# Sparse attention and a gated mixture layer on one core: seven products instead of eight in the outputs of two superblocks, and one written order for all engines

## The chip, the cores and the metric

The kernel runs on one core of one Trainium2 chip. The metric is the device time of one execution in microseconds (us); lower is better. The core's engines are TensorE (PE in the profile, with its weight loads as PEld), VectorE (DVE), ScalarE (ACT), GpSimd (POOL) and SyncE (SP), which here only issues transfers. Each engine runs its own instructions in program order and waits for the others where it needs their data or a buffer.

## What is computed

Eight batches of eight heads of attention over 576 positions, with two masks, then a gated layer over all 4608 tokens of width 512.

```python
mask_local = (rel >= 0) & (rel < stride)                                   # heads 0 to 3, stride 32
mask_strided = (rel >= 0) & (pos[None, :] % stride == pos[:, None] % stride)  # heads 4 to 7
scores = np.where(masks[None, :, :, :], scores, -1000000000.0)
attn = np.exp(scores - np.max(scores, axis=-1, keepdims=True))
attn = attn / (np.sum(attn, axis=-1, keepdims=True) + 1e-09)
x = np.matmul(attn, v)                       # 4608 x 512, heads side by side
gate = 1.0 / (1.0 + np.exp(-(x @ w_gate)))   # w_gate, w_val 512 x 1536
out = gate * (x @ w_val) @ w_out             # w_out 1536 x 512
```

## The kernel before

**Precision.** A float32 matrix is kept as two fp32r parts: h, a rounded copy (a cast on ACT), and l, what is left (a subtraction on DVE or POOL). A product of two such matrices is three products of parts (h·h, h·l, l·h; `three`, L417, and `outs`, L448). A large product in this text is one matmul of 128x128 weights against 512 columns.

**First block.** Batch 0, 512 of its 576 tokens, goes through the layer by plain products: for each of the 12 chunks of 128 hidden units, gate and value (24 products) and outputs (12), 432 in all. Beside it the attention of batches 0 to 2 runs, and the weights come in: `load_weight` (token W) fetches them as 64-bit words, ACT and DVE turn the words into float32 (a, b: `upper_words` and `lower_words`; w: `whole`, L390 to L399, a shift and an addition), and u and l split them (L407, L410). The last 64 tokens of each batch, the rests, are put aside.

**Superblocks.** The remaining batches go in pairs: `SUPER = ((1, 2), (3, 4), (5, 6), (7, None))`, where None stands for the eight rests together; a block is 512 tokens. Per superblock the two blocks' inputs are combined into seven input matrices, and gate and value weights into seven mixes, as in Winograd's form of Strassen's method, so that two halves of the tokens and two halves of the features need seven products (P1 to P7) instead of eight. `pair_of_chunks` (L559) does this for six pairs of chunks: 14 steps of 6 large products, 84 steps and 504 products. The results are combined by DVE and ACT (L571 to L573, L589 to L591) into h1 and h2, the gated hidden values. Mixes are formed by `form_mix` (L502) in the first superblock, kept in DRAM and loaded again in the later ones into a ring of four tiles (`next_of_ring`).

**Outputs.** Then `group_of_outs` (L618) makes the outputs of the two blocks by plain products, in 8 groups of three chunks: `load_outs` (L604) loads the output weights of a group (1.5 MB, already split) into the same ring, `split_outs` (L611) splits the hidden values (L615 on ACT, L616 on DVE), and 12 products per chunk follow, tokens on the partitions: 48 steps of 6, 288 products. `store` (L455) copies the four results of a block from PSUM (L459 on DVE, L461 on ACT) and writes rows of 2 KB.

**What sets the order.** All code runs in one manual schedule, so each engine's instructions stand in the order in which the Python issues them. For the first block and the attention beside it the string `ORDER` gives one token for each action; its parts between bars belong to the first steps of the first superblock. From there on `superblock` plans: `put` enters an action before or beside one of 132 steps (`tick`). `FORM` says at which steps the mixes are formed, and one pair of heads of the next superblock's attention gets 14 steps, with `STEP` and `TURN_AT` (turnings of the probabilities, L261, eight a pair of heads). The inputs of the next superblock (`mix_input`, L345: T are sums at L353, h casts at L363, l rests at L365, L the same on POOL) come in the last steps of the outputs.

**Attention of a pair of heads:** scores on PE (L197), mask, maximum and difference on DVE, exponential on ACT (L227), sum, the addition of 1e-9 and the reciprocal (`inverse`), multiplication by it (L240), turning by blocks (L261) and weighing on PE (L289).

```python
    def outs(accs, h, w, first, last, start=0):
        hh, hl = h
        wh, wl = w
        for i, o in enumerate(accs, start):
            for n, (a, b) in enumerate(((hh, wh), (hh, wl), (hl, wh))):
                nc.tensor.matmul(o, a[:, i * P : (i + 1) * P], b, start=first and n == 0, stop=last and n == 2)
```

Here the hidden values are the matmul's weights and the output weights move, so the outputs come out by tokens.

Of the kernel before, what the change touches and what calls it, by code (L numbers as in the profile page):

```python
# [65 lines left out]
ORDER = """  # L66
Q00 Z00 Z01 C Q01 S00 C1 W0.0 F000 F100 S01 F200 W0.1 E00 F001 N000 Q02 a0.0 F101 b0.0 N100 F201 a0.1 W1.0 N200 E01
w0.0 T00 b0.1 P00 Q03 w0.1 u0.0 Z02 S02 N001 l0.0 u0.1 F002 a1.0 V00 l0.1 b1.0 N101 F102 N201 V01 F202 T01 w1.0 E02
W1.1 P01 N002 X00 u1.0 Z03 M0- W0.2 S03 H00 N102 l1.0 L00 F003 V02 R00 g0.1.0 a1.1 N302 X01 F103 b1.1 g0.0.0 H01 w1.1
a0.2 V03 T02 L01 b0.2 U1.1 P02 F203 W2.0 g0.1.1 R01 Z10 w0.2 X02 E03 N003 l1.1 W2.1 g0.0.1 H02 N103 g1.0.0 L02 U0.2  # L70
N203 Q11 R02 g0.1.2 a2.0 D0.2 g1.0.1 b2.0 T03 w2.0 a2.1 W1.2 g1.0.2 P03 g1.1.0 u2.0 Z11 X03 b2.1 l2.0 g1.1.1 H03 V11
g0.0.2 L03 g1.1.2 w2.1 a1.2 W2.2 g0.0.3 R03 b1.2 S11 U2.1 s0 w1.2 g1.0.3 W3.0 g1.1.3 F011 l2.1 g0.1.3 F111 Q13 g2.0
U1.2 a2.2 m0 b2.2 F211 s1 w2.2 x0 W3.1 a3.0 g2.1 E11 y0 D1.2 V10 U2.2 m1 b3.0 l2.2 N011 O0 x1 N111 s2 Y1 W3.2 w3.0
a3.1 O1 b3.1 N311 m2 u3.0 x2 W4.0 D3.0 a3.2 w3.1 b3.2 T11 g3.0 P11 W4.1 w3.2 u3.1 Z13 Y2 Q10 a4.0 D3.1 X11 s3 U3.2
b4.0 g3.1 H11 l3.2 V13 a4.1 R11 w4.0 b4.1 W4.2 S10 w4.1 u4.0 O2 W5.0 D4.0 u4.1 m3 D4.1 x3 F010 Q12 Y3 a4.2 g4.1 F110
b4.2 w4.2 a5.0 W5.1 F210 b5.0 S13 u4.2 w5.0 E10 W5.2 g4.0 F013 D4.2 u5.0 Q21 N010 a5.1 D5.0 O3 b5.1 N110 s4 F113 W6.0
N210 w5.1 a5.2 T10 b5.2 m4 g5.0 P10 W6.1 w5.2 x4 Z12 u5.1 y4 a6.0 D5.1 b6.0 S12 F213 s5 W6.2 w6.0 g5.1 E13 F012 U5.2
Q20 D5.2 u6.0 F112 a6.1 X10 D6.0 b6.1 a6.2 F312 m5 g6.0 H10 N013 W7.0 x5 N113 b6.2 w6.1 E12 W7.1 R10 w6.2 u6.1 O4 s6
# [838 lines left out]
```

## Time and profile before

| | |
|---|---|
| median of 3 runs | 962.56 us (960.55, 962.56, 964.04) |
| the profiled execution | 959.72 us, of which the span is 957.9 us |
| mean granted TensorE clock | 0.993 |
| moved by DMA | 212.83 MB, 222 GB/s over the span |
| transfers to landing, median | gate and value mixes (1 MB) 9.3 us, output weights (1.5 MB) 6.4 us, an output of 256 KB 2.4 us |
| table loads on ACT | 46 |

The span runs from the first to the last instruction; the time of an execution has something around it. A row of the groups of instructions gives line, engine, operation, out<-in by the program's names (hs are split hidden values, wo output weights, mix the mixes, pt turned probabilities), shapes and count, then busy time in us and mean ns of one, then the engine's idle time just before and what ended it. A row of the stretches gives the stretch, its length and the busy time (and instructions) of PE, PEld, DVE, ACT and POOL, the granted clock, the share of time the DMA engines were busy, and GB/s. Matmuls overlap in the pipeline, so a mean of 392 ns for one does not say that one starts every 392 ns.

### The profile page before, as it was taken

The numbers are of one execution on the slowest core, as the hardware profiler recorded it, in microseconds if no ns is written. First come the engines' busy times: TensorE is split into PE (matmuls) and PEld (weight loads), VectorE is DVE, ScalarE is ACT, GpSimd is POOL, SyncE is SP. The second block draws the span as 40 slices with busy tenths as digits, with TensorE's granted clock in tenths as the row PEclk, the third lists the DMA queues.
The fourth block names the chain that finished last, engine by engine and source line by source line (L and its number), as shares of the span: only waits on it lengthen the run. The fifth ranks groups of instructions, "written<-read, shape, count | busy, mean of one in ns | idle before, by whom it ended". The sixth has DMA issues, their size and how long they took to land.

```text
span 957.9 us, 18020 instructions
## 1 busy us (share of the span) xinstructions
PE 924.3 (96%) x7576; PEld 744.2 (78%) x7576; DVE 583.8 (61%) x900; ACT 436.2 (46%) x778; POOL 112.5 (12%) x120
## 2 busy tenths in 40 slices
PE   3999999999999999999999999999999999999997
PEld 3778777677777878888777788877888888888886
DVE  6789888888877575566668674666266122224221
ACT  4679776756564333454443243444344123333121
POOL 1341345364430000000000000000000000000000
PEclk9999999989999999999999999999999999999999
DMA  7788765655573576865525669455625585531563
GB/s 267 234 301 282 263 242 210 238 229 227 199 260 139 212 271 245 321 252 231 213 109 185 218 234 374 197 221 212 215 103 213 199 342 217 239 159 66 198 242 111
DMA packets 43825, 212.83 MB, mean 222 GB/s; under 512 B 8672, under 2 KB 9952, under 8 KB 33504
## 3 DMA queue, kind: packets, MB, share of 16 engines
q1 hardware_dynamic: 40544, 199.77, 55.7%
q10 hardware_dynamic: 3200, 11.91, 3.7%
q8 instruction: 60, 0.98, 0.4%
q14 instruction: 21, 0.17, 0.1%
HBM read 172.86 MB, written 38.80 MB: 221 GB/s over the span
## 4 chain that ended last, share of the span: by engine, by line
PE 75%; DVE 13%; ACT 6%; DMA 3%; issue 2%; POOL 1%; SPq 0%; DVEq 0%; ACTq 0%; POOLq 0%
PE o L420 30%; PE o L453 13%; PE g L420 6%; PE g L453 6%; PE v L453 6%; PE v L420 6%; PE x L289 3%; PE s L197 2%; DVE pt L261 2%; DMA first_x1h<-in_w_all 2%; DMA first_x1l<-in_w_all 1%; ACT L227 1%; ACT mix L532 1%; DVE hs L616 1%; DVE mix L537 1%
## 5 line engine op out<-in xcount | busy, mean ns | idle before, releaser
L453 PE MATMUL o<-wo,hs 128*128 128x512 f32 x576 | 148.2, 392 | 0.9 <-DVE ob L459 0.9
L453 PEld LDWEIGHTS o<-wo,hs 128*128 128x128 f32 x576 | 107.2, 188 | 26.6 <-DVE ob L459 2.3
L616 DVE TENSOR_TENSOR hs<-h,hs 128x512 fp32r<-128x512 f32 x96 | 63.9, 688 | 104.4 <-ACT hs L615 104.2
L572 DVE TENSOR_TENSOR h<-s,o 128x512 f32<-128x512 f32 x48 | 32.9, 685 | 98.9 <-PE o L420 96.9
L615 ACT CAST hs<-h 128x512 fp32r<-128x512 f32 x96 | 55.3, 618 | 74.6 <-PE o L453 47.4
L261 DVE STREAM_TRANSPOSE pt<-sb 32x320 f32<-32x320 f32 (+1 forms) x160 | 85.8, 536 | 4.8
L453 PE MATMUL g<-wo,hs 128*128 128x512 f32 x288 | 81.9, 393 | 0.0
L573 ACT ACTIVATE s<-s 128x512 f32<-128x512 f32 x48 | 30.4, 633 | 111.7 <-DVE s L571 111.7
L453 PE MATMUL v<-wo,hs 128*128 128x512 f32 x288 | 81.0, 389 | 0.0
L420 PE MATMUL o<-x,mix 128*128 128x512 f32 x288 | 71.8, 397 | 0.2 <-ACT vq L591 0.2
L420 PE MATMUL o<-x0h,mix 128*128 128x512 f32 x192 | 67.6, 413 | 3.9 <-DVE ob L459 2.0
L420 PEld LDWEIGHTS o<-x,mix 128*128 128x128 f32 x288 | 52.9, 188 | 15.5 <-ACT s L573 3.2
L420 PE MATMUL o<-x2h,mix 128*128 128x512 f32 x192 | 64.5, 397 | 0.4
L420 PE MATMUL o<-x3h,mix 128*128 128x512 f32 x192 | 63.3, 390 | 0.3 <-DVE h L572 0.3
L420 PE MATMUL o<-x6h,mix 128*128 128x512 f32 x192 | 63.0, 389 | 0.0
L453 PEld LDWEIGHTS v<-wo,hs 128*128 128x128 f32 x288 | 54.1, 188 | 11.4
L453 PEld LDWEIGHTS g<-wo,hs 128*128 128x128 f32 x288 | 53.4, 188 | 11.2
L589 ACT COPY o<-o 128x512 f32<-128x512 f32 x48 | 27.4, 572 | 76.2 <-PE o L420 76.2
L231 DVE TENSOR_REDUCE mx<-sb 128x10 f32<-128x640 f32 (+1 forms) x26 | 21.3, 819 | 48.5 <-ACT sb L227 48.5
L420 PEld LDWEIGHTS o<-x0h,mix 128*128 128x128 f32 x192 | 37.4, 195 | 13.4 <-DVE ob L459 2.1
L573 ACT ACTIVATE s<-o 128x512 f32<-128x512 f32 x48 | 28.7, 598 | 34.8 <-PE o L420 34.6
L420 PEld LDWEIGHTS o<-x2h,mix 128*128 128x128 f32 x192 | 36.7, 191 | 9.4 <-ACT gq L591 1.7
(177 smaller groups left out, 1803.2 us busy)
## 6 DMA issues: line engine op xcount, KB each, us to landing
wo<-outer SPq DMA_DIRECT2D x32, 1536.0 KB, 6.4
mix<-mix SPq DMA_DIRECT2D x36, 1024.0 KB, 9.3
mix<-mix SPq DMA_DIRECT2D x36, 768.0 KB, 7.1
mix<-mix SPq DMA_DIRECT2D x12, 1792.0 KB, 6.0
first_x1h<-in_w_all SPq DMA_DIRECT2D x18, 512.0 KB, 4.7
first_x1l<-in_w_all SPq DMA_DIRECT2D x18, 512.0 KB, 4.6
out<-ob SPq DMA_DIRECT2D x32, 256.0 KB, 2.4
qk<-in_qk_l SPq DMA_DIRECT2D x11, 592.0 KB, 6.1
```

The source lines that it names most:

```text
L197: nc.tensor.matmul(sc[g * m : (g + 1) * m, j * BANK + s * kk : j * BANK + (s + 1) * kk], qk[d, q0 : q0 + m], qk[d, k0 : k0 + kk], start=Tr ...
L227: nc.scalar.activation(prob, prob, AF.Exp, scale=SCALE)
L231: nc.vector.tensor_reduce(row, prob, axis=AX.X, op=ALU.add)
L261: nc.vector.transpose(dst[to : to + LB, :, col : col + LB], src[rows : rows + LB, :, h * LB : (h + 1) * LB])
L289: nc.tensor.matmul(xp[j * D : (j + 1) * D, r * BANK + (u * per + g) * m : r * BANK + (u * per + g + 1) * m], v[rows, (u * per + g) * P + j ...
L420: nc.tensor.matmul(o, w, x, start=first and n == 0, stop=last and n == len(todo) - 1, skip_group_check=onto)
L453: nc.tensor.matmul(o, a[:, i * P : (i + 1) * P], b, start=first and n == 0, stop=last and n == 2)
L572: mul = lambda to, x, y: nc.vector.tensor_tensor(to, x, y, op=ALU.mult)
L573: sig = lambda to, x: nc.scalar.activation(to, x, AF.Sigmoid)
L589: P1=(g1, v1, lambda: nc.scalar.copy(g2, g1), lambda: nc.scalar.copy(v2, v1), True),
L615: nc.scalar.copy(hh, src)
L616: nc.vector.tensor_tensor(hl, src, hh.bitcast(F32), op=ALU.subtract)
```

## The change

1. **Outputs by seven products.** In the third and fourth superblocks (`BY_PARTS = (2, 3)`) `outs_by_parts` takes the place of `group_of_outs`. The hidden values of a pair of chunks are four matrices (A, B, C, D: two chunks by two blocks); `sum_of_h` makes the differences in place, and seven products, each in three stages of two pairs of chunks, give four quarters of the outputs: 7 x 3 x 2 steps of 6 products, 252. A stage is a ring tile with the output weights of one product (`load_stage`, two transfers of 256 KB) and the split hidden values (`split_stage`: casts on ACT, differences on DVE or POOL). The weights are now the stationary side and the hidden values move, so results come out with output columns on the partitions; DVE turns them in 32x32 blocks (`done`) and `store_turned` writes pieces of 256 bytes, four transfers a quarter for a batch and eight for the rests. The columns of `w_out` are permuted on the host (`turned`) so that turned blocks of 32 give whole runs; the plain `store` undoes the permutation in its copies (`runs`).
2. **Sums of the output weights.** `form_outs` makes the sums that the products need (tokens @l to @k: load, add up the halves, sums, casts, rests, keep), three pairs of chunks during the gates of the second superblock and three during those of the third, in the tiles of hidden chunks that are not yet written, and keeps them in DRAM.
3. **One written order.** `ORDERS` holds four texts, one for each superblock (the first with the first block ahead), with one part between bars for each step of six products; the planner (`FORM`, `STEP`, `TURN_AT`, `put`) goes. A token with @ is a step that the planner placed before; the last figure of @j and @T chooses DVE or POOL. The order of the first block is another one too.
4. **Smaller edits.** `inverse` becomes two steps (`safe`, `inverse`), and `whole` two (`shift`, `whole`); `load_mix` two transfers with places of their own; the temporary tiles are joined in twos; Q and V transfers from the fourth batch on go by SP's queue.

In the texts the attention beside the second superblock (batches 5 and 6) stands in steps 68 to 132 of 132, the first scores beside step 70; before, a pair of heads began every 14 steps from the first step on.

```diff
 SUPER = ((1, 2), (3, 4), (5, 6), (7, None))
+BY_PARTS = (2, 3)
+STAGE = 2
+STAGES = PAIRS // STAGE
+TURNED = 4
+OUT_SUMS = dict(P5=0, P6=1, P7=2, P3=3)
+OUT_PLAIN = dict(P1=(0, 0), P2=(1, 0), P4=(1, 1))
...
-ORDER = """
...
-X22 e3 e0 M1lt e2 e1 H22 | M1va R22 JT1 X23 M1vs Jh1 | M1ld H23 Jl1 R23 M1k S30 JT3 Jh4 | F030 Jh5 JT2 | Jl5 Jh3 | M2-
...
+ORDERS = (
+    """
...
+@J3.l2 @G2.16 @i2.16.0 @g2.16.1 @i2.16.1 | @T1.4.0 @g2.16.0 @G2.17 @i2.17.1 @j2.16.0.1 @i2.17.0 @g2.17.0 | @j2.16.1.1
...
+        def safe():
+            prob, row, by_row = rows()
+            nc.vector.tensor_scalar_add(row, row, 1e-9)
...
+    def shift(f, i):
+        high = words[f, i][0]
+        nc.vector.tensor_scalar(high, high, 3, None, op0=ALU.logical_shift_left)
...
+            (nc.vector.tensor_copy if i % 2 else nc.scalar.copy)(runs(ob, "a q"), runs(accs[i], "q a"))
...
-    def split_outs(s, n, q):
+    def split_outs(n, q, part, engine=None):
         j, g = divmod(n, GROUPS // 2)
         src = hs[g * THREE + q][:, j * TB : (j + 1) * TB]
         hh, hl = (hold["h", n][:, (2 * q + k) * TB : (2 * q + k + 1) * TB] for k in range(2))
-        nc.scalar.copy(hh, src)
-        nc.vector.tensor_tensor(hl, src, hh.bitcast(F32), op=ALU.subtract)
+        if part == 0:
+            nc.scalar.copy(hh, src)
+        else:
+            engine.tensor_tensor(hl, src, hh.bitcast(F32), op=ALU.subtract)
...
+    def form_outs(what, p, *args):
...
+        if what == "s":
+            t["st"] = flat("st", 4 * PART, f"sums_out{p}")
+            of = [t["st"][:, n * PART : (n + 1) * PART] for n in range(4)]
+            a11, a21, a12, a22 = (t["w"][:, n * PART : (n + 1) * PART] for n in range(4))
+            tt = (nc.gpsimd, nc.vector)[args[0]].tensor_tensor
+            tt(of[0], a21, a22, op=ALU.add)
+            tt(of[1], of[0], a11, op=ALU.subtract)
+            tt(of[2], a11, a21, op=ALU.subtract)
+            tt(of[3], a12, of[1], op=ALU.subtract)
+            return
...
+    def load_stage(n, q):
+        which, p = ORDER_OF_PARTS[n // STAGES], n % STAGES * STAGE + q
+        at = STAGE * 2 * TB + q * 2 * PART
+        to = hold["stage", n][:, at : at + 2 * PART].bitcast(F32)
+        if which in OUT_SUMS:
+            at = OUT_SUMS[which] * 2 * PART
+            nc.sync.dma_start(to, sums_out[p][:, at : at + 2 * PART])
+        else:
+            odd, half = OUT_PLAIN[which]
+            f = 2 * p + odd
+            src = outer[f // THREE][:, f % THREE * 2 * DM : (f % THREE + 1) * 2 * DM]
+            src = src.rearrange("p (k n) -> p k n", k=2)[:, :, half * PART : (half + 1) * PART]
+            nc.sync.dma_start(to.rearrange("p (k n) -> p k n", k=2), src)
...
+    SPLIT_OF = dict(P1="A", P5="B", P6="B", P2="C", P7="A", P3="D", P4="B")
...
+    def split_stage(n, q, part, engine=None):
...
+        if part == 0:
+            nc.scalar.copy(h, src)
+        else:
+            engine.tensor_tensor(l, src, h.bitcast(F32), op=ALU.subtract)
...
+    def sum_of_h(p, m, engine):
+        a, b, c, d = (part_of_h(p, x) for x in "ABCD")
+        to, x, y = ((b, b, a), (b, d, b), (a, b, a), (b, c, b))[m - 1]
+        engine.tensor_tensor(to, x, y, op=ALU.subtract)
...
+    def store_turned(t, b, half, split):
+        for a in range(TURNED):
+            src = t[a * LB : (a + 1) * LB]
+            cols = slice(a * P + half * REST, a * P + (half + 1) * REST)
+            queue = nc.scalar if split and a % 2 else nc.sync
+            if b is not None:
+                to = out[b * S : b * S + TB, cols].rearrange("(m i) n -> i m n", i=LB)
+                queue.dma_start(to, src.rearrange("p (m n) -> p m n", n=REST))
...
+    def outs_by_parts(s, banks, tick):
+        (a1, a2, a5), (b1, b2, b5) = banks
+        one, two, five = (a1, b1), (a2, b2), (a5, b5)
...
+        def done(which, n, b, half, src, d):
...
+            nc.vector.transpose(to, src.rearrange("p (m j) -> p m j", j=LB))
...
+        after = dict(
+            P1=lambda d: nc.scalar.copy(two[d], one[d]),
+            P5=lambda d: keep("p", "t4", five, d),
+            P6=lambda d: keep("q", "t3", two, d),
+            P2=lambda d: done("P2", 0, 0, 0, one[d], d),
+            P7=lambda d: done("P7", 1, 1, 1, add("p", two, d), d),
+            P3=lambda d: done("P3", 2, 1, 0, add("q", five, d), d),
+            P4=lambda d: done("P4", 0, 0, 1, two[d], d),
+        )
+        into = dict(P1=one, P5=five, P6=two, P2=one, P7=two, P3=five, P4=two)
...
+            for k in range(STAGES):
+                t = hold.pop(("stage", i * STAGES + k))
+                for d in range(2):
+                    with tick():
+                        todo = []
+                        for q in range(STAGE):
+                            w, h = STAGE * 2 * TB + q * 2 * PART + d * P, 2 * q * TB
+                            wh, wl = (t[:, w + m * PART : w + m * PART + P] for m in range(2))
+                            todo.append(((wh, wl), (t[:, h : h + TB], t[:, h + TB : h + 2 * TB])))
+                        three(into[which][d], todo, fresh and k == 0, k == STAGES - 1, onto=not fresh)
+                    if k == STAGES - 1:
+                        after[which](d)
...
-                args = (nc.sync if b == 0 and (kind == "Q" or p < 2) or (b, p) == (BY_PE, 1) else nc.scalar,)
+                early = b == 0 and (kind == "Q" or p < 2)
+                args = (nc.sync if early or (b, p) > (BY_PE, 0) else nc.scalar,)
...
-    FORM = (
...
-    STEP = ((1, "F1"), (2, "F2"), (3, "E"), (5, "N0"), (6, "N1"), (6, "N2"))
-    TURN_AT = (7, 8, 9, 10, 11, 12, 13, 14)
...
+        def steps():
+            for what in order[clock[0]]:
+                step(what)
+            clock[0] += 1
...
+        if parts:
+            outs_by_parts(s, banks, tick)
+        else:
+            for n in range(GROUPS):
+                group_of_outs(s, n, banks, tick)
...
+    turned = w_out.reshape(DF, TURNED, TURNED, LB).transpose(0, 2, 1, 3)
-    w_all = np.stack([wg, wv, w_out.reshape(NF, P, DM)], 2).view(np.int64)
+    w_all = np.stack([wg, wv, turned.reshape(NF, P, DM)], 2).view(np.int64)
```

**TensorE, the outputs of the third superblock.** The rows are line, operation, out<-in with the tile's number, size and count; g, v, o_0 and o_1 are PSUM banks, wo and hs the loaded weights and split hidden values of a group. Before, a run in the change from the first group to the second:

```order
L453 MATMUL g3_5935<-wo3_0_6918,hs3_0_6917 128x512 x3
L453 MATMUL v3_5936<-wo3_0_6918,hs3_0_6917 128x512 x3
L453 MATMUL o3_0_5933<-wo3_0_6918,hs3_0_6917 128x512 x3
L453 MATMUL o3_1_5934<-wo3_0_6918,hs3_0_6917 128x512 x3
L453 MATMUL g3_5935<-wo3_1_7039,hs3_1_7038 128x512 x3
L453 MATMUL v3_5936<-wo3_1_7039,hs3_1_7038 128x512 x3
```

After, from the start of the same outputs (stage is a ring tile with weights and hidden values):

```order
L530 MATMUL o3_0_5931<-stage3_0_6773 128x512 x6
L530 MATMUL o3_1_5932<-stage3_0_6773 128x512 x6
L396 MATMUL x7_2_7011<-pt7_2_6912,vv7_2_6909 64x32 x36
L530 MATMUL o3_0_5931<-stage3_1_6796 128x512 x6
L530 MATMUL o3_1_5932<-stage3_1_6796 128x512 x6
L530 MATMUL o3_0_5931<-stage3_2_6982 128x512 x6
L530 MATMUL o3_1_5932<-stage3_2_6982 128x512 x6
L530 MATMUL g3_5933<-stage3_3_6997 128x512 x6
L530 MATMUL v3_5934<-stage3_3_6997 128x512 x6
L530 MATMUL g3_5933<-stage3_4_7048 128x512 x6
```

Each step's six products now go into one bank from one stage instead of two banks of three, and the weighings of batch 7 (x7) stand between them.

**VectorE, the fourth pair of chunks of the second superblock.** h2, s22, s12 and o2 are hidden values, gate sums and PSUM of that superblock; sb5, mx5 and pt5 belong to the attention of batch 5. Before:

```order
L219 TENSOR_REDUCE mx5_3_4673<-sb5_3_4672 128x12
L223 TENSOR_TENSOR sb5_3_4672<-sb5_3_4672,mx5_3_4673 128x12x54
L231 TENSOR_REDUCE mx5_3_4673<-sb5_3_4672 128x12
L235 TENSOR_SCALAR mx5_3_4673<-mx5_3_4673 128x12
L236 RECIPROCAL mx5_3_4673<-mx5_3_4673 128x12
L240 TENSOR_TENSOR sb5_3_4672<-sb5_3_4672,mx5_3_4673 128x12x54
L261 STREAM_TRANSPOSE pt5_3_4819<-sb5_3_4672 32x12x32
L572 TENSOR_TENSOR h2_6_4670<-s11_2_3_4811,o2_1_4062 128x512
```

After:

```order
L693 TENSOR_TENSOR h2_6_4446<-s11_2_3_4501,o2_1_4030 128x512
L692 TENSOR_TENSOR s22_2_3_4517<-o2_0_4029,gp_2_3_4469 128x512
L692 TENSOR_TENSOR s22_2_3_4517<-o2_1_4030,gp_2_3_4469 128x512
L692 TENSOR_TENSOR s12_2_3_4534<-g2_4031,gq_2_3_4484 128x512
L693 TENSOR_TENSOR h2_7_4447<-s22_2_3_4517 128x512
L692 TENSOR_TENSOR s12_2_3_4534<-v2_4032,gq_2_3_4484 128x512
L693 TENSOR_TENSOR h2_6_4446<-s12_2_3_4534 128x512
L693 TENSOR_TENSOR h2_7_4447<-s11_2_3_4501,o2_1_4030 128x512
```

The fourth pair of heads stood among the gates here; now the gates and values follow each other and the attention comes later.

**VectorE, the end of the outputs of the third superblock.** ob are copied outputs, turned3_P4 a turned quarter, raw and x inputs of the fourth superblock. Before:

```order
L616 TENSOR_TENSOR hs3_6_7305<-h3_6_6542,hs3_6_7305 128x512
L616 TENSOR_TENSOR hs3_6_7305<-h3_7_6543,hs3_6_7305 128x512
L616 TENSOR_TENSOR hs3_6_7305<-h3_8_6749,hs3_6_7305 128x512
L616 TENSOR_TENSOR hs3_7_7350<-h3_9_6750,hs3_7_7350 128x512
L616 TENSOR_TENSOR hs3_7_7350<-h3_10_6909,hs3_7_7350 128x512
L616 TENSOR_TENSOR hs3_7_7350<-h3_11_6910,hs3_7_7350 128x512
L459 COPY ob6_1_7434<-o3_1_5934 128x512
L459 COPY ob6_3_7440<-v3_5936 128x512
L572 TENSOR_TENSOR h4_0_7447<-s11_4_0_7507,o4_1_7444 128x512
L571 TENSOR_TENSOR s22_4_0_7522<-o4_0_7443,gp_4_0_7475 128x512
```

After:

```order
L829 TENSOR_TENSOR stage3_20_7462<-h3_10_6777,stage3_20_7462 128x512
L460 TENSOR_TENSOR raw7_5950<-raw_rest_7236,raw7_5950 128x1024
L460 TENSOR_TENSOR raw_rest_7236<-raw_rest_7236 128x1024
L866 STREAM_TRANSPOSE turned3_P4_7528<-o3_0_5931 128x16x32
L472 TENSOR_TENSOR x5_4_7525<-raw_rest_7236,x5_4_7525 128x1024
L460 TENSOR_TENSOR raw7_5950<-raw_rest_7236,raw7_5950 128x1024
L460 TENSOR_TENSOR raw7_5950<-raw7_5950 128x1024
L866 STREAM_TRANSPOSE turned3_P4_7528<-o3_1_5932 128x16x32
L693 TENSOR_TENSOR h4_0_7558<-s11_4_0_7616,o4_1_7555 128x512
L692 TENSOR_TENSOR s22_4_0_7631<-o4_0_7554,gp_4_0_7584 128x512
```

The differences of split hidden values stand alone before; after, one of them is followed by sums of the next inputs (L460), a rest (L472) and two turnings (L866) up to the last product.

More of the change, by code (lines that the diff above doesn't have):

```diff
@@ L64 @@
 }
-ORDER = """
[L67 to L76, printed above, removed]
@@ new lines, in sum_of_h @@
+    def sum_of_h(p, m, engine):
[10 more added lines that the diff above has]
+                queue.dma_start(to, src.rearrange("p (m n) -> p m n", n=REST))
+            else:
+                to = out.rearrange("(m r) n -> r m n", r=S)[TB:, :, cols]
+                for k in range(REST // LB):
+                    src_k = src.rearrange("p (m k n) -> p k m n", k=REST // LB, n=REST)[:, k]
+                    queue.dma_start(to[k * LB : (k + 1) * LB], src_k)
@@ L691, in step, with later_step @@
         elif kind == "e":
-            store(acc[0], 0, OBS[0], [int(of)])
+            store(acc[0], 0, ("t0", "t1", "t2", "t3"), [int(of)])
+    def later_step(kind, args):
+        if kind == "J":
+            mix_input(int(args[0]), args[1])
+            return
+        if kind == "O":
+            store_turned(*turned.pop(args[1]))
+            return
+        args = [int(x) for x in args if x]
+        engines = nc.vector, nc.gpsimd
+        if kind == "A":
+            room_of_mix(*args)
+        elif kind == "L":
+            load_mix(*args)
+        elif kind == "H":
+            load_outs(*args)
+        elif kind == "G":
+            room_of_stage(*args)
+        elif kind == "g":
+            load_stage(*args[1:])
+        elif kind in "ij":
+            split = split_stage if args[0] in BY_PARTS else split_outs
+            split(args[1], args[2], int(kind == "j"), engines[args[3]] if kind == "j" else None)
+        elif kind == "T":
+            sum_of_h(args[0], args[1], engines[args[2]])
+        elif kind == "R":
+            raw[None] = flat("raw_b", NC * TB, "raw_rest")
+            for m in range(B):
+                to = raw[None].rearrange("p (c n) -> p c n", c=NC)[:, :, m * REST : (m + 1) * REST]
+                nc.sync.dma_start(to, rests[m].rearrange("p (c n) -> p c n", c=NC))
+        else:
+            form_outs(kind, *args)
     forms = {}
@@ L807, in superblock @@
+    def superblock(s):
+        parts = s in BY_PARTS
+        order = [part.split() for part in ORDERS[s].split("|")]
         two = [bank(f"o{m}", f"o{s + 1}_{m}") for m in range(2)]
```

336 lines of the change are left out of this document (205 added, 131 removed).

## The prediction

> **What bounds the kernel now.** I read the page first: engine totals, then the chain that ended last.
>
> ```profile
> span 957.9 us, 18020 instructions
> PE 924.3 (96%) x7576; PEld 744.2 (78%) x7576; DVE 583.8 (61%) x900; ACT 436.2 (46%) x778; POOL 112.5 (12%) x120
> PE 75%; DVE 13%; ACT 6%; DMA 3%; issue 2%; POOL 1%; SPq 0%; DVEq 0%; ACTq 0%; POOLq 0%
> ```
>
> TensorE is in use almost throughout and is three quarters of the chain. A busy PE need not be a PE at its pace, so I took the pace from one piece of the chain in order of time, six large products in an undisturbed place, and then the busy times of each engine stage by stage. The columns are stretch, length, PE, weight loads, DVE, ACT, POOL (instructions in brackets), granted clock, DMA share and GB/s. I cut the stretches where the first block ends and where each superblock (a pair of batches) passes from its gate and value products to its outputs; the last row is what comes after the last product.
>
> ```profile
> 710.77 1.36 PE o L453 x6
> ```
> ```profile
> 0.00:163.80 163.80, 143.80 (x1925) 114.11 (x1925) 136.59 (x217) 118.33 (x221) 57.40 (x56) 1.00 0.75 258
> 163.80:306.00 142.20, 137.24 (x1317) 108.34 (x1317) 115.52 (x177) 84.70 (x154) 53.71 (x58) 0.97 0.54 210
> 306.00:379.60 73.60, 72.06 (x581) 57.89 (x576) 49.09 (x72) 24.86 (x47) 0.40 (x2) 1.00 0.67 248
> 379.60:508.90 129.30, 129.30 (x1201) 103.49 (x1192) 84.67 (x140) 59.57 (x100) 0.40 (x2) 1.00 0.56 217
> 508.90:582.60 73.70, 72.16 (x584) 57.92 (x577) 49.13 (x72) 24.86 (x47) 0.40 (x2) 1.00 0.67 249
> 582.60:706.40 123.80, 123.80 (x915) 100.15 (x913) 69.12 (x112) 52.25 (x92) 0.20 (x1) 1.00 0.56 211
> 706.40:772.20 65.80, 65.80 (x291) 53.99 (x289) 28.65 (x36) 20.31 (x32) 0.00 (x0) 1.00 0.61 224
> 772.20:886.40 114.20, 114.20 (x505) 94.59 (x504) 34.41 (x51) 37.94 (x66) 0.00 (x0) 1.00 0.49 193
> 886.40:952.10 65.70, 65.70 (x289) 53.72 (x288) 15.90 (x25) 12.78 (x23) 0.00 (x0) 1.00 0.50 184
> 952.10:957.90 5.80, 0.19 (x1) 0.00 (x0) 0.69 (x1) 0.59 (x1) 0.00 (x0) 0.78 0.61 182
> ```
>
> 1.36 us for six is 0.2267 us each. A superblock has 504 + 288 = 792 such products, 179.5 us. The fourth superblock (the two rows from 772.20) takes 179.9: it has no attention beside it and loses nothing. The third takes 189.6; the 9.7 more are the scores and weighings of four pairs of heads, 2.4 us a pair. The second, with eight pairs, takes 203.0 where 179.5 + 19.4 = 198.9 would do; the first takes 215.8 and loses 17. The first block needs 432 products, 97.9 us, plus twelve pairs, about 29, and takes 163.8: there DVE (136.6) and ACT (118.3) are nearly as full as PE. So from 379.6 on the time is the number of products; before that it is partly waits.
>
> **Fewer products.** The program's order shows 252 products where 288 stood in the outputs of the third and fourth superblocks: 42 steps of six instead of 48. That is 72 x 0.2267 = **-16.3 us**, all of it on PE where PE waits for nothing. It stands if the new work of the other engines stays hidden; the rest of this part is what hides it.
>
> **The work that feeds the products.** These are groups of instructions (line, engine, operation, out<-in, count; busy time, mean ns; idle before and its releaser).
>
> ```profile
> L616 DVE TENSOR_TENSOR hs<-h,hs 128x512 fp32r<-128x512 f32 x96 | 63.9, 688 | 104.4 <-ACT hs L615 104.2
> L615 ACT CAST hs<-h 128x512 fp32r<-128x512 f32 x96 | 55.3, 618 | 74.6 <-PE o L453 47.4 <-PE v L453 26.8
> L261 DVE STREAM_TRANSPOSE pt<-sb 32x384 f32<-32x384 f32 x80 | 45.6, 570 | 2.5
> L261 DVE STREAM_TRANSPOSE pt<-sb 32x320 f32<-32x320 f32 x80 | 40.2, 503 | 2.3
> L353 DVE TENSOR_TENSOR raw<-raw 128x1024 f32<-128x1024 f32 x7 | 9.0, 1290 | 0.5 <-ACT raw L320 0.4
> L365 DVE TENSOR_TENSOR x<-raw,x 128x1024 fp32r<-128x1024 f32 x6 | 7.3, 1218 | 0.0
> L412 POOL TENSOR_TENSOR w<-whole,w 128x512 fp32r<-128x512 f32 x9 | 11.9, 1333 | 27.8 <-ACT w L408 27.6
> ```
> ```profile
> wo<-outer SPq DMA_DIRECT2D x32, 1536.0 KB, 6.4
> ```
>
> ACT: 42 casts x 0.618 = 26 us in 57 us of products, with copies still far below PE. Loads: 42 of 256 KB (11.0 MB) a superblock where eight of 1536 KB (12.6 MB) were, asked for three or four stages (8 to 11 us) ahead against 6.4 us for six times the size. Both cost nothing; uncovered, a late stage would cost what it is late, a few us. The sums of the output weights are formed while the second and third superblocks make gates, where DVE has 40 us to spare; their stores end before the fourth pair of blocks writes the borrowed tiles. Also nothing, and 2 to 3 us if one store is late.
>
> DVE and POOL are the tight ones. A turned output is 512 elements; from 503 and 570 ns for 320 and 384 I estimate 704. A pair of attention heads costs DVE (69.12 + 28.65 - 34.41 - 15.90 - 13.7) / 4 = 8.5 us, the third superblock's DVE less the fourth's and less 4 x 1.29 + 7 x 1.22 for the next input sums and their rests (L353, L365). Counting the order by these prices:
> - last 42 steps of the third superblock: 57.1 + 2.4 = 59.5 us of PE; DVE 39 differences x 0.69 + 9 small turnings x 0.54 + 8 input sums and rests of about 1.25 + 8 turned outputs x 0.70 + 4 additions x 0.69 = 50; POOL 17 x 1.33 + 3 x 2.4 = 30 (2.4 us is the POOL row below).
> - last 56 steps of the second: 76.2 + 7 x 2.4 = 93 us of PE, because seven of eight attention pairs now stand there; DVE 7 x 8.5 + 24 = 84; POOL 13 x 1.33 + 5 x 2.4 = 29.
> - last 42 of the fourth: 57.1 us of PE; DVE 37, POOL 19. No excess.
>
> Alone each engine fits. Together they don't always run, as the order of time near 158 us shows:
>
> ```profile
> 157.61 0.42 DVE L525 TENSOR_TENSOR sums<-whole 128x256 f32<-128x256 f32 x1
> 158.00 2.40 POOL L365 TENSOR_TENSOR x2l<-raw,x2h 128x1024 fp32r<-128x1024 f32 x1 [2.96 <-ACT x2h L363]
> 158.06 2.61 DVE L526 TENSOR_TENSOR sums<-sums,whole 128x256 f32<-128x256 f32 x1
> ```
>
> The same subtraction took 0.42 us and, begun beside a POOL instruction, 2.61: it ended when POOL ended. [...]
>
> DVE plus POOL exceed PE by 20 us in each of the first two lists, 40 in all. The nearest row is 163.80:306.00, where 115.5 + 53.7 exceed 142.2 by 27 and PE lost 5.0, with about 3 more at half clock (below): 0.3 per us. Of the 40, some 8 at each superblock's end can run on into the next one's first steps, where DVE has little. So (40 - 16) x 0.3 = **+7 us**; bounds 0 and 40. A gain from these moves is excluded, as PE waits for nothing there now.
>
> **Waits before 379.6 that the order may move.** The largest waits of PE in 163.80:306.00 (us, times, longest), and what follows one:
>
> ```profile
> PE x L289 <- DVE pt L261: 2.2, 2, 1.8
> PE o L420 <- DVE ob L459: 2.0, 1, 2.0
> PE o L420 <- ACT s L573: 1.9, 1, 1.9
> ```
> ```profile
> 188.50:190.70 2.20, 0.33 (x25) 0.20 (x15) 0.72 (x3) 2.17 (x4) 0.00 (x0) 1.00 0.37 122
> 190.70:194.00 3.30, 3.30 (x8) 2.62 (x9) 3.23 (x8) 1.25 (x3) 0.75 (x2) 0.50 0.27 105
> ```
>
> In the second row eight products fill 3.3 us where fifteen would fit: the granted clock fell to 0.50 after 2 us of wait, so that wait cost 2 + 1.6. [...] Three waits and two such dips are 6.1 + 3.2 = 9.3 us. The order splits the two weight steps and the two reciprocal steps apart and groups ACT's functions (9 table loads for 13 in the first superblock), so some of this goes; I take a third, **-3 us**. Bounds: -12 with the smaller waits, +6 if the first block's other order waits as much anew, which no row excludes.
>
> **The end.** The last product and what follows it now, then the nearest rows for 256-byte pieces:
>
> ```profile
> 951.45 0.84 PE L453 MATMUL v<-wo,hs 128*128 128x512 f32 x3
> 952.33 0.69 DVE L459 COPY obNone<-v 128x512 f32<-128x512 f32 x1 [0.67 <-PE v L453]
> 953.01 1.39 ACTq L467 DMA_DIRECT2D out<-obNone  x2
> ```
> ```profile
> L801 SPq DMA_DIRECT2D raw_rest<-rests x8: 628/630/2524, 672.5 to 680.0; - x8
> DMA to landing us min/median/max: 2.7/5.0/6.8
> ```
>
> Now the last product ends at 952.29 and the program 5.6 us later. After: one turning (0.70), two issues on each queue (0.63, then 0.63), 5.0 to land, about 7.0: **+1.4 us**, bounds -1 and +3. The turned stores also pass SP's queue inside the outputs; 0.63 us an issue, four to eight of them, beside stage loads asked for 8 us ahead, cost nothing unless DVE is late with a turning, when the loads behind wait as long: part of the crowding above.
>
> **Sum.** -16.3 + 7 - 3 + 1.4 = -10.9. The profiled execution took 959.7 (span 957.9 and 1.8 around it), so 948.8; the median of the runs, 962.6, lies 2.8 above it: **951.7 us**.
>
> **Rivals.**
> [...]
> - [...] PE waits for the differences in the last 42 and 56 steps. All 40 us on PE: -16.3 + 1.4 + 40 - 3 = +22, 985 us; with 22.5 of them +4.6, 967 us. It decides from 17.9 us, 45% of the excess, where the nearest row shows 30%. For it: one 2 us wait costs 3.6. Against: stages are prepared 8 us ahead, so short delays vanish.
> - *Nothing left.* The excess costs 15 to 20 us and eats the gain: about 962.6.
> - That the change doesn't do what it says is out: the order has the 72 products fewer.
>
> **Chances.** Forecast 0.62 (own range 944 to 959), both gains 0.19, nothing left 0.09, lock 0.10. This kernel's runs tell about 0.3%, 2.9 us, from no change: faster 0.81, same 0.09, slower 0.10. The range, 936 to 964, leaves out the lock and little else: its low end is the first rival with the waits at -12 (-16.3 + 1.4 - 12 = -26.9, 935.7), its high end the excess at 20 us.
>
> **What would show it.** Outputs of the third and fourth superblocks in 57 to 60 us each with PE full: the first term right. PE waits on stage differences (DVE or POOL) near the ends of the second and third, and clock dips there: the crowding, with its size. [...] First product of the first superblock later than 163.8 us: the first block's order is worse. The forecast is wrong if the fourth superblock's outputs exceed 60 us, or if waits before 380 us change by over 8.

## The result, and the profile after

The changed kernel takes **969.12 us** (median of 5 runs, 967.26 to 971.5) beside 963.08 for the kernel before (5 runs): a ratio of 1.0064, 95% interval 1.0041 to 1.0088. It is slower by some 6 us; 951.7 was forecast, faster, and 969.1 lies above the range.

The head of the changed kernel's page and its chain, to be put beside those of before:

```profile
span 967.8 us, 18484 instructions
PE 912.4 (94%) x7504; PEld 733.7 (76%) x7504; DVE 609.6 (63%) x964; ACT 453.0 (47%) x820; POOL 242.1 (25%) x202
PE 84%; DVE 8%; ACT 4%; DMA 2%; issue 1%; SPq 1%; POOL 1%; ACTq 0%; DVEq 0%
```

PE is busy 11.9 us less than before in a span that is 9.9 us longer: the products are fewer, and PE stands still for some 22 us more. Where it stands still, the stretches of the changed kernel show. They are cut as before, and once more wherever PE waits at the end of a superblock:

```profile
0.00:165.10 165.10, 146.01 (x1969) 115.64 (x1969) 124.42 (x213) 118.88 (x230) 62.39 (x62) 1.00 0.76 256
165.10:295.20 130.10, 127.52 (x1073) 101.94 (x1073) 102.40 (x168) 76.68 (x137) 40.73 (x40) 1.00 0.58 222
295.20:370.50 75.30, 74.74 (x697) 59.52 (x695) 47.17 (x79) 24.68 (x49) 14.31 (x11) 1.00 0.67 236
370.50:377.50 7.00, 0.00 (x0) 0.00 (x0) 4.55 (x3) 1.53 (x3) 4.76 (x3) 0.68 0.72 300
377.50:498.10 120.60, 120.55 (x632) 98.04 (x633) 51.04 (x78) 47.07 (x77) 16.88 (x15) 0.98 0.66 248
498.10:581.30 83.20, 83.18 (x1137) 65.73 (x1135) 71.22 (x120) 28.53 (x61) 25.53 (x19) 1.00 0.75 266
581.30:591.80 10.50, 0.00 (x1) 0.00 (x0) 9.24 (x7) 5.61 (x12) 2.75 (x2) 0.66 0.48 176
591.80:717.40 125.60, 124.64 (x876) 100.43 (x877) 69.99 (x120) 54.91 (x92) 18.18 (x15) 0.99 0.69 247
717.40:781.80 64.40, 61.83 (x375) 49.96 (x373) 52.53 (x69) 30.61 (x56) 27.44 (x18) 1.00 0.77 229
781.80:787.50 5.70, 0.05 (x1) 0.00 (x0) 2.17 (x3) 1.63 (x2) 2.34 (x1) 0.88 0.87 367
787.50:904.10 116.60, 116.54 (x498) 95.34 (x499) 37.45 (x54) 38.71 (x67) 7.94 (x5) 0.98 0.45 172
904.10:961.40 57.30, 57.30 (x253) 47.11 (x252) 36.69 (x54) 24.16 (x43) 18.86 (x14) 1.00 0.68 202
```

Three short rows hold next to no product (0.05 us of PE at most): 7.0, 10.5 and 5.7 us, each where a superblock ends. PE's waits name who ended them:

```profile
PE o L530 <- ACT ob L577: 17.6, 2, 10.5
PE o L530 <- DVE turned_P L866: 5.7, 1, 5.7
```

L577 is the copy of outputs out of PSUM and L866 the turning of outputs. The next superblock's first product (x0h) needs their bank. Here is what stands ahead of those copies, rows chosen in the order of time at the second end:

```profile
580.40 0.91 PE L396 MATMUL x<-pt,vv 54*64 54x54 f32 x44
581.35 0.71 ACT L427 COPY raw<-x 128x288 f32<-128x288 f32 x3 [6.30 <-PE x L396]
582.16 1.23 DVE L460 TENSOR_TENSOR raw<-raw,raw 128x1024 f32<-128x1024 f32 x1 [4.07 <-ACT raw L427]
583.31 1.22 DVE L472 TENSOR_TENSOR x<-raw,x 128x1024 fp32r<-128x1024 f32 x1
584.44 1.22 DVE L460 TENSOR_TENSOR raw<-raw 128x1024 f32<-128x1024 f32 x1
585.58 1.22 DVE L472 TENSOR_TENSOR x3l<-raw,x3h 128x1024 fp32r<-128x1024 f32 x1
586.82 2.34 POOL L472 TENSOR_TENSOR x<-raw,x 128x1024 fp32r<-128x1024 f32 x1 [9.29 <-ACT x L470]
586.83 3.40 DVE L460 TENSOR_TENSOR raw<-raw 128x1024 f32<-128x1024 f32 x1
590.16 0.68 DVE L577 COPY ob<-o 128x512 f32<-128x512 f32 x1
590.27 1.04 ACT L470 CAST x6h<-raw 128x1024 fp32r<-128x1024 f32 x1 [3.53 <-DVE raw L460]
591.22 0.58 ACT L577 COPY ob<-o 128x512 f32<-128x512 f32 x1
591.70 0.59 ACT L577 COPY ob<-g 128x512 f32<-128x512 f32 x1
591.85 0.80 PE L530 MATMUL o<-x0h,mix 128*128 128x512 f32 x1 [10.55 <-ACT ob L577]
```

The last weighing of attention (L396) ends with the last product. Only then can the chain of the next inputs begin: sum, rest, sum, rest, sum on DVE, with casts on ACT between. The last output product ends by 580.5, so the copies could run then; but they stand behind that chain on both engines and start 9.7 and 10.7 us later. In these rows the copy at 590.16 passed nothing of the chain: it starts as the sum written ahead of it, 3.40 us from 586.83, ends.

At the third end the chain is late for another reason. The last weighing there (batch 7) had ended by 733.6, 48 us earlier. In DVE's order the chain's later steps stand between the turnings of the last two outputs, and the first turning can't begin before PE's last products:

```profile
779.17 0.72 DVE L866 STREAM_TRANSPOSE turned_P<-o 128x512 f32<-128x512 f32 x1 [2.40 <-PE o L530]
783.28 2.34 POOL L472 TENSOR_TENSOR x3l<-raw,x3h 128x1024 fp32r<-128x1024 f32 x1 [4.20 <-ACT x3h L470]
785.66 1.23 DVE L460 TENSOR_TENSOR raw<-raw 128x1024 f32<-128x1024 f32 x1 [3.53 <-POOL x3l L472]
786.80 0.71 DVE L866 STREAM_TRANSPOSE turned_P<-o 128x512 f32<-128x512 f32 x1
```

The place of the last copies and turnings, behind late steps of the chain, is the same at all three ends.

After each wait the clock is at half for a while (a product every 0.43 us instead of 0.2267 at first, and a mean granted clock of 0.58, 0.67 and 0.55); the stretches just behind:

```profile
377.50:384.50 7.00, 6.95 (x19) 5.47 (x20) 0.00 (x0) 1.63 (x4) 2.10 (x2) 0.58 0.88 309
591.80:596.50 4.70, 4.65 (x14) 3.74 (x15) 0.00 (x0) 1.22 (x3) 2.10 (x2) 0.67 0.82 271
787.50:793.50 6.00, 5.94 (x15) 4.74 (x16) 0.01 (x1) 1.93 (x4) 2.37 (x1) 0.55 0.73 164
```

In these 17.7 us 48 products start where 78 would at 0.2267; the 30 that are missing cost 30 x 0.2267 = 6.8 us. The waits are 7.08 + 10.55 + 5.71 = 23.3; together **30.1 us** at three places. By this estimate the kernel without them would be near 939.

### The profile page after: what moved, and what is told of

Its sections match the earlier page's. It is cut to its first block, busy times and chain, and to the rows that moved or that the text cites. A ratio compares the mean times of both kernels' runs of the same rounds, so it can differ in the third digit from the quotient of the medians.

```text
span 967.8 us, 18484 instructions
## 1 busy us (share of the span) xinstructions
PE 912.4 (94%) x7504; PEld 733.7 (76%) x7504; DVE 609.6 (63%) x964; ACT 453.0 (47%) x820; POOL 242.1 (25%) x202
## 4 chain that ended last, share of the span: by engine, by line
PE 84%; DVE 8%; ACT 4%; DMA 2%; issue 1%; SPq 1%; POOL 1%; ACTq 0%; DVEq 0%
PE o L530 38%; PE g L530 11%; PE v L530 11%; PE o L563 10%; PE x L396 3%; PE g L563 3%; PE v L563 3%; PE s L301 3%; DVE pt L368 1%; DVE raw L460 1%; DVE s L692 1%; PE t L355 1%; DVE h L693 1%; DMA first_x1h<-in_w_all 1%; DVE mix L655 1%
## 5 line engine op out<-in xcount | busy, mean ns | idle before, releaser
L530 PE MATMUL o<-stage 128*128 128x512 f32 x360 | 83.5, 390 | 2.6 <-DMA stage<-outer 1.6
L530 PEld LDWEIGHTS o<-stage 128*128 128x128 f32 x360 | 67.3, 188 | 17.4 <-DMA stage<-outer 2.0
L829 POOL TENSOR_TENSOR stage<-h,stage 128x512 fp32r<-128x512 f32 x29 | 40.3, 1403 | 149.9 <-ACT stage L827 115.8
L563 PE MATMUL o<-wo,hs 128*128 128x512 f32 x288 | 75.6, 397 | 0.5 <-DVE ob L577 0.5
L739 POOL TENSOR_TENSOR hs<-h,hs 128x512 fp32r<-128x512 f32 x23 | 30.6, 1352 | 155.4 <-ACT hs L737 155.4
L827 ACT CAST stage<-h 128x512 fp32r<-128x512 f32 x84 | 48.0, 621 | 38.8 <-issue 17.9
L563 PEld LDWEIGHTS o<-wo,hs 128*128 128x128 f32 x288 | 52.5, 188 | 13.9 <-DVE ob L577 1.2
L710 ACT COPY o<-o 128x512 f32<-128x512 f32 x48 | 27.4, 571 | 60.7 <-PE o L530 60.6
L829 DVE TENSOR_TENSOR stage<-h,stage 128x512 fp32r<-128x512 f32 x55 | 44.1, 828 | 10.3 <-ACT stage L827 9.3
L692 DVE TENSOR_TENSOR s<-o,gp 128x512 f32<-128x512 f32 x48 | 33.1, 690 | 25.6 <-PE o L530 25.5
L737 ACT CAST hs<-h 128x512 fp32r<-128x512 f32 x48 | 26.9, 620 | 33.7 <-PE o L563 25.5
```

The lines of the kernel that those rows point to most:

```text
L530: nc.tensor.matmul(o, w, x, start=first and n == 0, stop=last and n == len(todo) - 1, skip_group_check=onto)
L692: add = lambda to, x, y: nc.vector.tensor_tensor(to, x, y, op=ALU.add)
L710: P1=(g1, v1, lambda: nc.scalar.copy(g2, g1), lambda: nc.scalar.copy(v2, v1), True),
L739: engine.tensor_tensor(hl, src, hh.bitcast(F32), op=ALU.subtract)
L827: nc.scalar.copy(h, src)
L829: engine.tensor_tensor(l, src, h.bitcast(F32), op=ALU.subtract)
```

## The experiments

All medians are of runs beside the kernel before, whose own median was 962.3 to 963.1 in them. **The order theory:** copies and turnings of the last outputs stand behind the input chain, and PE waits for their bank. **Its rival**, called the lock in the chances and the expectations: DVE is slowed beside POOL (in the kernel before, L526 took 2.61 us beside a POOL rest and 0.42 elsewhere on DVE), and the chain is just too long.

**1. The chain behind the copies.** The last parts of the first three orders (the second is shown); the part behind the new bar runs after the copies:

```diff
-| X63 H63 V70 @J2.T2 @J2.h4 @J2.l4 @J2.h3 @L0.1.1 @J2.T3 R63 @J2.l3 @J2.h5 @J2.T4 @J2.L5 @J2.h6 @J2.L6
+| X63 H63 V70 @L0.1.1 R63
+| @J2.T2 @J2.h4 @J2.l4 @J2.h3 @J2.T3 @J2.l3 @J2.h5 @J2.T4 @J2.L5 @J2.h6 @J2.L6
```

> The changed kernel with the input steps (sums, casts and rests of the next superblock's inputs) of the last part of the first three orders moved behind the copies or turnings of the last outputs. Theory of the order (the output copies stand behind the input chain on ACT and DVE, so TensorE waits for its banks): the three waits of 7.1, 10.6 and 5.7 us at the superblocks' ends shrink to 1 to 3 us each, but the chain now stands ahead of the first copies of the next superblock on ACT, so up to 5 us a boundary may come back: 943 to 958 us. Rival (DVE is slowed by POOL, the chain is simply too long): the same waits appear a few steps later, for the inputs: 962 to 970 us.

Measured: 954.59 us (ratio 0.9912, 0.9891 to 0.9934), 14.5 less than the changed kernel. Of the three waits at most 1.5 us each is left, and two new ones have come:

```profile
PE o L530 <- ACT o L710: 6.7, 2, 4.3
```

L710 is ACT's copy of the first product of the next superblock: it now stands behind the chain's casts. As the order theory had it.

**2. The chain spread.** The steps up to the third input's rest stay behind the copies, the others go beside the fourth step of the next superblock:

```diff
+| @J2.T2 @J2.h4 @J2.l4 @J2.h3 @J2.T3 @J2.l3
...
-|
+| @J2.h5 @J2.T4 @J2.L5 @J2.h6 @J2.L6
```

> As the run before, but only the chain up to the third input's rest stands right behind the output copies; the steps after it (for the fourth to sixth inputs, which are needed 9 to 13 steps later) stand beside the fourth step of the next superblock. Theory of the order: the three waits and the half clock after each go, about 23 less 2 or 3 for copies that can't be hidden, and 6 to 8 of half clock: 938 to 946 us. Rival (chain too long, POOL slow): at least 955 us.

Measured: 950.31 us (0.9866, 0.9842 to 0.989), 18.8 less than the changed kernel and below the kernel before. That is 4 us above the expected range and 5 below the rival's: the mechanism holds, some waits stay (the longest of them 2.8 us, in the first pair of chunks of the third superblock; runs 9 and 12).

**3. The same order with less POOL.** `@J…L` becomes `@J…l` for 12 rests in the last steps of the first three orders:

```diff
-@J2.L5 @J2.h6 @J2.L6
+@J2.l5 @J2.h6 @J2.l6
```

> The changed kernel with its order, but the rests of the next inputs in the last steps of the first three orders (12 instructions) on VectorE instead of GpSimd. Theory of the order: only the chain gets shorter (2.35 us on POOL become 1.2, two sums of 3.4 beside POOL become 1.2), waits at the ends shrink by 2 to 4 us each and stay: 957 to 964 us. Rival (the lock between VectorE and GpSimd takes the gain): 938 to 948 us.

Measured: 962.95 us (1.0009, 0.9988 to 1.003), 6.2 less than the changed kernel. The time is in the range of the order theory. The waits are still there, shorter at the first two ends and longer at the third:

```profile
PE o L530 <- ACT ob L577: 10.9, 2, 8.3
PE o L530 <- DVE turned_P L866: 6.9, 1, 6.9
```

The first end's wait fell from 7.1 to 2.6 us, so there POOL was the larger part of it; the second fell from 10.6 to 8.3, the third rose from 5.7 to 6.9. POOL made the chain dearer, by some 6 us in the kernel's time; without it 17.8 us of waits remain, so it isn't the main cause.

**4. Only the place in the order, in the kernel before.**

```diff
-                put(at + n * 2 // 3, mix_input, s + 1, what)
+                put(ALL - 1, mix_input, s + 1, what)
```

> The kernel before with all its input steps for the next superblock in the last step of the outputs, ahead of the last output copies; nothing of it is on POOL. Theory of the order: 4 sums and 7 rests of DVE, 13.7 us, and casts between them stand ahead of the copies, TensorE waits 11 to 17 us at each of three ends, with 1.6 of half clock: 998 to 1015 us. Rival (lock): without POOL the chain is hidden again or costs little: 963 to 975 us.

Measured: 964.83 us (1.0009, 0.999 to 1.0028): no wait at the first two ends and 1.0 us at the third. The expectation missed by 33 us, the time lies in the rival's range, and the theory had to be mended: standing last in the program alone made nothing late. In the kernel before the last weighing was 22 steps back, the splits of the last group were done, and DVE and ACT could go through the chain while PE was at its last products, as the missing waits show. What makes the chain late is that it *can't start*: in the changed kernel the last weighing stands in the last step at the first two ends, and at the third the chain's later steps stand behind a turning that waits for PE. Run 5 tests the late weighing against the rival; the third end's reason was not tried apart.

**5. The place and the late weighing, in the kernel before.** The weighing of the eighth pair of heads goes to the last step but one, at two of the three ends:

```diff
-                x = at + (WEIGH_LATE if late and at >= FIRST else WEIGH)
+                x = ALL - 2 if late and at >= FIRST else at + WEIGH
...
-                put(at + n * 2 // 3, mix_input, s + 1, what)
+                put(min(at + n * 2 // 3, ALL - 1), mix_input, s + 1, what)
```

> The kernel before, with the weighing of the last pair of heads in the first and second superblocks moved to the last step but one (from step 110), and the input steps for the next superblock behind it in the last step, ahead of the output copies. Refined theory (the chain of input steps can't begin before the last weighing, and the copies stand behind it): TensorE waits 10 to 15 us at two ends, with 1.6 us of half clock each: 985 to 998 us. Rival (position in the order matters little, VectorE and ScalarE run ahead, as with the inputs alone in the last step; what costs in the changed kernel is GpSimd): 963 to 972 us.

Measured: 992.91 us (1.0315, 1.0264 to 1.0365), 30.1 us slower than before: in the expected range, and above the rival's.

```profile
PE o L420 <- ACT ob L461: 25.4, 2, 12.7
```

Two waits of 12.7 us for the output copies, with no POOL instruction in the chain, and a lower clock behind each: the next gates have a mean granted clock of 0.98 and take 132.0 and 126.3 us, where the kernel before has 1.00 and takes 129.3 and 123.8. It is the changed kernel's stall, made in the kernel before by two lines.

**6. The late weighing, chain behind the copies.** Only the first line of run 5's edit; the old formula then puts all but two input steps behind the copies.

> As the run before, but all input steps after the first two stand behind the output copies. Refined theory: the copies are no longer late; the first products of the next superblock run and then wait a few us for their inputs and for ACT, 2 to 6 us at two ends: 967 to 978 us, at least 12 us less than the run before. Rival: no difference between the two.

Measured: 985.95 us (1.0223, 1.0187 to 1.0259), 7 less than run 5 where at least 12 were expected, and 8 above the expected range. The wait has moved from one instruction of ACT to another. The output copies are in time, and now ACT's copy of the next superblock's first product stands behind the chain's casts, as in run 1:

```profile
PE o L420 <- ACT o L589: 13.8, 2, 6.9
```

So in the kernel before a late weighing costs either way, and the place of the output copies is the smaller part of it. In the changed kernel run 2 keeps the chain's later steps out of ACT's way too; the same was not tried here.

**7. What the seven products bring.** Run 2's kernel with `BY_PARTS = ()`: groups of plain outputs in the third and fourth superblocks, placed as the planner of before did, no sums of output weights.

```diff
-BY_PARTS = (2, 3)
+BY_PARTS = ()
...
-| F172 @G2.0 @g2.0.1 @i2.0.1
-| @i2.0.0 @j2.0.1.1 @g2.0.0 B71.4
+| F172
+| @H2.0 B71.4
```

> The kernel of the run with spread input steps (950.3 us), with the outputs of the third and fourth superblocks by plain products again, 288 for 252 in each, and without the sums of output weights; the rest of the order is the same. Theory of the products (72 at 0.2267 us, all of them on TensorE's path): 13 to 18 us slower, 963 to 968 us. Rival (the work around the seven products, differences, turnings and loads, eats half of it): 953 to 960 us.

Measured: 956.77 us (0.9932, 0.9904 to 0.9961), only 6.5 more than run 2; 13 to 18 were expected, and the time lies in the rival's range. Outputs of the third and fourth superblocks, first with plain products (run 7), then by seven (run 2):

```profile
697.30:766.30 69.00, 68.31 (x405) 55.69 (x404) 28.30 (x41) 20.12 (x37) 2.41 (x1) 1.00 0.68 237
883.70:950.00 66.30, 66.08 (x289) 53.62 (x287) 15.91 (x25) 12.73 (x23) 0.00 (x0) 1.00 0.50 183
```
```profile
703.20:766.00 62.80, 60.48 (x369) 48.93 (x368) 50.62 (x67) 30.60 (x56) 27.41 (x18) 1.00 0.76 223
884.40:941.70 57.30, 57.30 (x253) 47.11 (x252) 36.42 (x54) 24.17 (x43) 18.86 (x14) 1.00 0.67 202
```

6.2 + 9.0 = 15.2 us in the outputs themselves, near the 16.3 of the sum. So 8 or 9 us come back elsewhere.

**8. Attention of the second superblock ten steps earlier**, in run 2's kernel, with its input chain (last weighing in step 122 of 132), so that the chain runs beside the last products:

```diff
-| @L5.1.0
+| @L5.1.0 S50
...
-| B62.1 @i1.7.2 @j1.7.1.1 B62.2 @i1.7.0 S63 B62.3 @j1.7.2.1 B62.4
+| @i1.7.2 @j1.7.1.1 @i1.7.0 @j1.7.2.1 X63 H63 V70 R63 @J2.T2 @J2.h4 @J2.l4 @J2.h3
```

> The kernel of the run with spread input steps, with all attention of the second superblock and its input steps 10 steps earlier (the last weighing at step 122 of 132 instead of 132), so that the chain runs beside the last products. Theory of the late weighing: the waits of 1.5 and 2.8 us at the start of the third superblock go: 945 to 949 us. Rival (VectorE is full there, the work only moves): 949 to 953 us.

Measured: 952.05 us (0.9883, 0.9836 to 0.993): no gain. It is the rival's case, the work only moves. At the start of the third superblock the waits of 1.5 and 2.8 us became one of 1.4, but in the second PE now waits 1.9 us for a turning and 2.2 for a load of queries and keys.

**9. Run 2 with run 3's edit.**

```diff
-@J2.h5 @J2.T4 @J2.L5 @J2.h6 @J2.L6
+@J2.h5 @J2.T4 @J2.l5 @J2.h6 @J2.l6
```

> The kernel with spread input steps (950.3 us), with the rests of the next inputs in the last steps on VectorE instead of GpSimd, as was done to the changed kernel alone. Theory of the order (the chain is shorter by 1.2 us a rest, and the wait of 2.8 us at the start of the third superblock goes): 945 to 949 us. Rival (with the copies ahead of it the chain is hidden, so its engine no longer matters): 949 to 952 us.

Measured: 950.32 us (0.9884, 0.9848 to 0.9921), the same as run 2. What was worth 6 us with the copies behind the chain is worth nothing with the copies ahead: POOL's price was paid only through that wait.

**10. The sums alone.** Run 7's kernel, with the tokens of `form_outs` put back; the sums are formed and stored, and nobody reads them.

```diff
-| @A2.1.0 @A2.1.1 Z71 Z70
+| @A2.1.0 @A2.1.1 Z71 Z70 @l3
...
-| @L1.1.1
-|
-|
+| @L1.1.1 @w3.0.0
+| @w3.1.0
+| @s3.1
```

> The kernel with plain outputs everywhere (956.8 us), with the sums of the output weights formed and stored all the same (nobody reads them). The seven products saved 15.2 us in the two outputs by the profile, and 7.5 of it came back elsewhere. If the sums beside the gates of the second and third superblocks cost it: 959 to 963 us. If they are hidden, as the prediction had it, and the cost comes with the inputs and stages: 955 to 958 us.

Measured: 963.2 us (1.001, 0.9993 to 1.0027), 6.4 more than run 7. Gates of the third superblock, without the sums (run 7), then with them (run 10):

```profile
571.30:697.30 126.00, 124.83 (x877) 100.49 (x878) 66.53 (x107) 54.86 (x88) 4.99 (x3) 0.99 0.57 214
```
```profile
574.70:705.60 130.90, 126.15 (x876) 101.19 (x877) 73.14 (x122) 58.23 (x94) 15.17 (x11) 0.97 0.70 254
```

And where PE waits in run 10's first pair of chunks there, in the order of time:

```profile
586.50 2.52 POOL L763 TENSOR_TENSOR whole_out<-split 128x512 f32<-128x512 f32 x2 [0.95 <-DMA split<-outer]
589.05 0.42 DVE L753 TENSOR_TENSOR sums_out<-whole_out 128x256 f32<-128x256 f32 x1 [8.15 <-POOL whole_out L763]
590.52 0.68 DVE L674 TENSOR_TENSOR h<-s,o 128x512 f32<-128x512 f32 x1
591.26 1.22 PE L511 MATMUL o<-x,mix 128*128 128x512 f32 x2 [3.80 <-DVE h L674]
```

DVE has 73 of 131 us to do, and yet it stands for 8.15 us: its next instruction is a sum that waits for POOL, which had two rests of inputs to do and then waited 0.95 us for a load. Behind it stands the hidden value (L674) whose PSUM bank PE needs. In run 9, where these rests are on DVE, PE's longest wait for a hidden value is 2.8 us, as in run 2; so POOL's rests don't set the time, and the load is left as the cause.

**11. The chain at the third end five steps earlier**, on run 9's kernel; that weighing (batch 7) is long done.

```diff
-| @j2.17.0.0 @J3.l0 @G2.19 @g2.19.1 @i2.19.1
+| @j2.17.0.0 @J3.l0 @G2.19 @g2.19.1 @i2.19.1 @J3.T1
...
-| @J3.T1 @O2.P3 @A3.0.1
-| @J3.h1 @J3.T3
+| @O2.P3 @A3.0.1 @J3.T2
+| @J3.l5 @J3.h3
```

> The first kernel of this call, with the input chain at the end of the third superblock's outputs begun five steps earlier, its last weighing being long done. Theory of the order: the waits of 1.6 and 0.9 us at the start of the fourth superblock go, 1 to 3 us less than the first kernel. Rival (VectorE is full with differences there and these come late instead): the same or up to 3 us more.

Measured: 953.56 us (0.9911, 0.9878 to 0.9943), 3.2 more than run 9, as the rival said; the intervals overlap.

**12. The sums three steps later**, in run 2's kernel and the third superblock:

```diff
-| @w3.0.0 @L1.1.1
-| @w3.1.0
-| @s3.1
-| @l4
+| @L1.1.1
+|
+|
+| @w3.0.0
```

> The kernel with spread input steps (950.3 us), with the steps on the sums of the output weights in the third superblock three steps later (their first load stays). Theory from the run with sums and plain outputs (VectorE waits for GpSimd's additions, which wait for the load, and TensorE's next hidden value stands behind them): the wait of 2.8 us in the first pair of chunks and the half clock after it go, 3 to 5 us: 945 to 947.5 us. Rival (the sums cost by their number, not by this wait): 949 to 951 us.

Measured: **946.08 us** (0.9829, 0.9808 to 0.985), 4.2 less than run 2; its slowest execution, 947.21, is below the fastest of run 2, 947.99. The wait of 2.8 us is gone, the longest of its kind is now 1.0. The gates of the third superblock:

```profile
574.30:700.00 125.70, 123.79 (x876) 99.03 (x877) 76.29 (x126) 58.36 (x96) 20.39 (x15) 1.00 0.71 261
```

125.7 us where run 2 had 128.5, with the same work. This version beats both kernels: 1.7% below before, some 23 us below the changed one.

## Why the prediction was wrong

The ledger of medians, each row one difference:

| from | to | us |
|---|---|---|
| kernel before (962.8) | run 7: the new order, at most 1.5 us of wait at an end, no seven products | -6.0 |
| run 7 | run 10: sums of the output weights | +6.4 |
| run 10 | run 2: 36 products fewer in each of two outputs | -12.9 |
| run 2 | changed kernel: input chain ahead of the last copies | +18.8 |

- **-16.3 for fewer products: right**, and nearly all on PE's path: 15.2 in the outputs by the profiles, 12.9 by the medians of runs 10 and 2. The fourth superblock's outputs took 57.3 us, as the last part asked for. The third's row is 64.4, above its 57 to 60: products and weighings make 59.4, seven products of the next superblock 1.6, and PE idles 2.6.
- **+7 for crowding of DVE and POOL: the step that failed.** The step counted an excess of work in the last steps of the second and third superblocks; the end of the first was not on its list. That DVE's and POOL's work adds up throughout was the author's estimate from the rows near 158 us, and no run shows it. The excess within the outputs cost little: in 717.40:781.80 PE idles 2.6 us, in 498.10:581.30 next to nothing. What failed is the sentence that some 8 us of excess at each end "can run on into the next one's first steps, where DVE has little". I looked at how much DVE had to do there and not at what stands behind it in the queue: the copies that free PE's banks. Most of the work itself could be hidden, as run 2 shows; the copies behind it are 6 to 11 us late: 30.1 us of wait and half clock by the profile where the term had 7. Run 2, with the same work in another order, is 18.8 us faster.
- **The slower rival (lock, 0.10, in the chances) foresaw the sign and not the place.** That its 967 us is near the measured time is luck. It had PE waiting for the differences in the last 42 and 56 steps; in the two rows named above PE idles 2.6 us in all. DVE was slowed beside POOL (a sum of 1.22 us took 3.40 beside a rest of 2.34), and moving 12 of POOL's rests to DVE, which also shortens each rest from 2.35 to 1.2 us, is worth 6.2 us in the changed kernel (run 3) and nothing when the copies go first (run 9). The prediction's row of 0.42 us is an addition (L525) and not the same subtraction (L526); but L526 takes 0.42 elsewhere on DVE, so the reading of the 2.61 stands.
- **Both gains (0.19 in the chances, and the low end of the range): no run shows them without crowding.** -16.3 + 1.4 - 12 was the author's estimate; the changed kernel took 969.12 us, and run 12, the fastest, 946.08.
- **"Also nothing" for the sums: wrong by 6.4 us** (run 10, with plain outputs). In the kernel with seven products a later place in the third superblock alone gives 4.2 back (run 12). DVE's 40 us of spare time were real; an engine with time to spare still blocked when its next instruction waited (8.15 us in run 10).
- **-3 for waits before 379.6: right in sign, too small.** The first superblock's gates and outputs took 142.2 + 73.6 = 215.8 and now 130.1 + 75.3 = 205.4, 10.4 less. Of this, 2.6 us are scores and weighings that stand elsewhere now (19.5 us of PE's time there before, 16.9 after). Beside 179.5 for its products it lost 16.8 and now loses 9.0, so 7.8 us went; but at its end stands the new wait of 7.1. In its gates PE's idle time fell from 5.0 to 2.6 us and the granted clock rose from 0.97 to 1.00. Which part of the new order did it was not tried. The first block's time hardly changed: 163.8 and 165.1, and 162 to 166 in the runs that share its new order.
- **+1.4 for the end: about right.** The last turning starts at 961.46 and the span ends at 967.8, 6.3 us, where 5.6 followed the last product before and 7.0 were forecast: +0.7 for +1.4.
